# A one-core linear-attention and squared-ReLU block: reordered head loads, merged rest loads, gates moved and woven

## The chip, the core and the metric

The kernel runs on one core of one Trainium2 chip. The metric is device time in microseconds (us) of one execution; lower is better. Everything is bfloat16 in memory, with fp32 sums. The engines that appear below are TensorE (PE; its weight loads are PEld), VectorE (DVE), ScalarE (ACT), GpSimd (POOL) and SyncE (SP). SP and ACT issue DMAs.

## What is computed

x has 2048 tokens of width 448. From the normalised tokens xn two branches are made and multiplied:

```python
xn = _layernorm(x)
# branch A: linear attention, 16 heads of width 28
q, k, v = split(xn @ wqkv)
phi = lambda t: jnp.where(t > 0, t + 1, jnp.exp(t)) + 1e-6
pq, pk = phi(q), phi(k)
kv = einsum("bhsd,bhse->bhde", pk, v)
z = einsum("bhsd->bhd", pk)
o = einsum("bhqd,bhde->bhqe", pq, kv) / (einsum("bhqd,bhd->bhq", pq, z)[..., None] + 1e-6)
s = o @ wo
# branch B: 448 -> 1792 -> 448
h = xn @ w1 + b1
g = silu(relu(h)**2 @ w2 + b2)
return x + s * g
```

## The kernel before, in words

**Tiles.** The 2048 tokens are 16 tiles of 128; four tiles make a group (0 to 3). The width 448 is cut into three full pieces of 128 and a rest of 64. The rest is kept twice, in partitions 0 to 63 and 64 to 127, so that two matmuls of 64 rows can run side by side in the two halves of the array. That is why each weight has a "main" load (three pieces) and "rest" loads (`load_rest`, L396: the same 64 rows of DRAM, copied once into each half by a DMA of its own).

**Units of work on TensorE.** K*i* is the k projection of token tile *i* (L605), Q*g.m* piece *m* of q for group *g* (L615), H*g.f* one of the 14 pieces of h for group *g* (L649), G*i* the gate of tile *i*, from all 14 pieces of h (L957 in halves of the array, L974 in the whole array), S*i* the attention output of tile *i* (L1007). `pe_four` (L523) takes four units a, b, c, d and issues them as pairs: (a, c), (b, d), then both again with the halves exchanged. A gate in such a group takes 14 steps in each half where the others take 4 and 3.

**Between the projections and the end.** R0, R1 are the rests of q (L720). A0 to A3 sum xn times pk over all tokens (L741, L747). `zsums` (L764) adds up pk over the tiles, half of the tiles on POOL and half on VectorE (L769, L781). Z turns that into columns (L794), D makes the denominators (L818). Then ACT takes their logarithm and exponential (lnd L828, rden L832), `spread` writes rden to DRAM (scr) and reads it back in 22 DMAs with each head's row repeated over its 28 partitions, into the space of xT; VectorE multiplies q by it in four instructions (L857 three times, L879 once). V folds the sums with wv (L893), its result goes through VectorE (kvm, L904), M folds that with wo (L919). Every S needs all four multiplies and M.

**Output of a tile.** VectorE adds b2 to the gate (L939), ACT applies silu (L995); gates 14 and 15 get b2 on TensorE and silu straight from PSUM (L956, L947). VectorE multiplies S by the gate (L1012), and the sum with x is on VectorE or POOL (L1017). SP issues the 16 output DMAs.

**Head.** LayerNorm of tile *i* is bn_stats and bn_aggr (L440, L441), two small ACT instructions (L448, L452), xn on VectorE (L459) and the second copy of the rest. Tiles 0 to 3 are transposed on TensorE (L502), with copies out of PSUM on VectorE and ACT (L514, L515); tiles 4 to 15 are transposed by DMAs on SP (L488), two tiles each. The first eight pieces of h of group 0 are accumulated tile by tile as the tiles and the pieces of w1 arrive: six of them in L665, two in L682, and the rests of all eight in L699. They occupy all eight PSUM banks. Dummy matmuls (L1032) run ahead of them.

**What sets the order.** TensorE and SP execute in the order in which the program adds their operations: TensorE's is written out by hand in the strings at the end, SP's is that of the `dma` calls. For ACT, VectorE and POOL a list scheduler in the kernel (`Program.schedule`) chooses the order from estimated durations, due times (`late`) and, for some operations, a choice of engine (`alts`). All engines then run their list strictly in order, with semaphores between them. One `dma` is one DMA instruction.

The strings that give TensorE's order:

```python
run(hs(0, 8, 12) + " P8 H0.12 H0.13 K0 K1 P12 Q0.0 K2 Q0.1 K3 Q0.2 K4 H1.0 H1.1")
run(hs(1, 2, 6) + " XG0,K5,G1,K6 " + hs(1, 6, 10) + " XG2,K7,G3,K8 " + hs(1, 10, 14))
...
run("R0 R1 A3 Z D I0,1,2,3,4,5,6,7 A0 A1 A2 G8 I8 V G9 I9 M")
run("XG10,S0,G11,S4 I10,11 XG12,S1,G13,S5 I12,13 S2 S3 S6 S7 XG14,S8,G15,S12 S9 S10 S13 S14")
run("S11 S15")
```

P is the LayerNorm and transposing of four tiles, I the silu of gates, X one `pe_four` of the units named.

Of the kernel before, what the change touches and what calls it, by code (L numbers as in the profile page):

```python
# [6 lines left out]
ALU = mybir.AluOpType  # L7
AF = mybir.ActivationFunctionType

P = 128  # L10
# [31 lines left out]
class Program:  # L42
# [27 lines left out]
    def schedule(self):  # L70
# [9 lines left out]
        for op in reversed(ops):  # L80
            late = 1e9
            for s in op.succ:
                late = min(late, s.ideal if s.eng == "pe" else s.late)
            for r in op.reads:
                if isinstance(r, Buf):
                    late = min(late, self.writer[r].ideal + 2.5)
            op.late = late - op.dur - LAT[op.eng] if op.prio is None else op.prio
# [40 lines left out]
        while n:  # L128
            best = None
            for e in self.ENGINES:  # L130
# [17 lines left out]
                else:  # L148
                    cands = []
# [12 lines left out]
                    for st, op in cands:  # L162
                        if op.alts:
                            mine = op.dur if op.eng == e else dict(op.alts)[e]
                            others = [(op.eng, op.dur)] + list(op.alts)
                            r = ready(op)
                            if any(
                                max(r, free[x]) + dx < st + mine - 1e-9 for x, dx in others if x != e
                            ):
                                continue  # L170
                            keep.append((st, op, mine))
                        else:
                            keep.append((st, op, op.dur))
# [92 lines left out]
def bass_recurrent_scan__linear_attn_block__dense_activation_squared_relu__prompt_kernel(  # L266
    nc, A_x, A_wqkv, A_wo, B_x, B_w1, B_b1, B_w2, B_b2, out
):
    with ExitStack() as es:
# [35 lines left out]
        zacc = sb("zacc", [P, 2, D], f32)  # L305
# [80 lines left out]
        def load_x(lo, hi, eng="sp"):  # L386
            dma(eng, x_tok[:, lo:hi, :], x_r[:, lo:hi, :], [("x", i) for i in range(lo, hi)], (hi - lo) * P * D * 2)
# [8 lines left out]
        def load_rest(eng, w, src, name, lo, hi, off=0):  # L396
            for i in (0, 1):
                dma(
                    eng, w[64 * i : 64 * i + 64, 3, lo:hi], src[384:448, off + lo : off + hi], [(name, 3 + i)],
                    64 * (hi - lo) * 2,  # L400
                )

        wn = lambda name: [(name, i) for i in range(5)]
# [3 lines left out]
        load_x(1, 2, "act")  # L407
        dma("act", b1r[:, :], B_b1.rearrange("(f p) -> f p", p=P), ["b1r"], F * 2)
        for c in range(3):
            load_main("sp", w_1, B_w1, "w1a", 0, WA, c, c + 1)  # L410
        load_x(2, 4)
# [82 lines left out]
        def pe_transpose(si, pieces):  # L494
            for lo, hi, eng in pieces:
                b = Buf("T")

                def f(e, _, lo=lo, hi=hi, b=b):
# [6 lines left out]
                add(  # L505
                    "pe", f, [("xn", si), "ident"] + ([("xd", si)] if hi == 4 else []), [b], 0.0558 * (hi - lo), mode="128",
                    label=f"T{si}.{lo}",
                )

                def ev(e, eng, lo=lo, hi=hi, b=b):  # L510
# [8 lines left out]
                    eng, ev, [b], [("xT", si, c) for c in range(lo, hi)] + ([("xT", si)] if hi == 4 else []),  # L519
                    0.15 + 0.07 * n if eng == "dve" else 0.18 + 0.107 * n, label=f"eT{si}.{lo}",  # L520
                ).prio = -1 if eng == "act" else None


        def pe_four(a, b, c, d):
            units = (a, b, c, d)
            half = (slice(0, 64), slice(64, 128))
            last = {}
            for us, second in (((a, c), False), ((b, d), False), ((c, a), True), ((d, b), True)):
                whole = us[0][6] > 4
                n = (us[0][6] if second else NF) if whole else 3 if second else 4  # L530
                cuts = [0, 7, n] if whole else [0, n]
                for lo, hi in zip(cuts, cuts[1:]):
# [8 lines left out]
                    reads, banks = [], [u[0] for u in us]  # L541
                    for u in us:
                        reads += [r for r in u[1] if r not in reads]
                    if whole:
                        reads = [r for r in reads if r[0] != "r2" or lo <= r[2] < hi]
                    op = add(
                        "pe", f, reads + (banks if second or lo else []), banks, (hi - lo) * MM(us[0][4]), mode="64",
                        label="+".join(u[5] for u in us) + ("'" if second else "") + (f".{lo}" if lo else ""),
                    )
                    if second and lo == 0:  # L550
                        op.sync = last[id(banks[0])]
                    last[id(banks[0])] = last[id(banks[1])] = op
                if second:
                    for u in us:
                        u[3]()

        def pe_two(a, b):
            half = (slice(0, 64), slice(64, 128))
            first = None
            for second, us in ((False, (a, b)), (True, (b, a))):  # L560
                n = 3 if second else 4

                def f(e, _, us=us, n=n, second=second):
                    for k in range(n):
                        for h in (0, 1):
                            m = us[h][2](e, half[h], k, k == 0 and not second, k == n - 1 and second)
                    return m

                banks = [u[0] for u in us]
                op = add(  # L570
                    "pe", f, a[1] + [r for r in b[1] if r not in a[1]] + (banks if second else []), banks, n * MM(a[4]), mode="64",
                    label=a[5] + "+" + b[5] + ("'" if second else ""),
                )
                if second:
                    op.sync = first
                    for u in us:
                        u[3]()
                first = op
# [97 lines left out]
        def head_rest():  # L676
# [15 lines left out]
            for lo in range(0, HW, 2):  # L692
# [13 lines left out]
                add("pe", f, [("xT", i) for i in range(4)] + [("w1a", 3), ("w1a", 4)] + bs, bs, MM(512), mode="64", label=f"Hr{lo}")  # L706
# [57 lines left out]
        def zsums():  # L764
            def acc(k, eng, tiles):
                for n, i in enumerate(tiles[1:]):
                    add(
                        eng,
                        lambda e, _, n=n, i=i: e.tensor_tensor(  # L769
                            out=zacc[:, k, :], in0=pk[:, tiles[0], :] if n == 0 else zacc[:, k, :], in1=pk[:, i, :], op=ALU.add  # L770
                        ),
                        [("pk", i), ("pk", tiles[0]), ("pk", 11)] if n == 0 else [("pk", i), ("zacc", k)], [("zacc", k)],
                        1.05 if eng == "pool" else 0.64, label=f"z{k}.{i}",
                    )

            acc(0, "pool", list(range(0, 8)))
            acc(1, "dve", list(range(8, 16)))
            for lo, at_, n in ((0, 0, D), (384, D, 64)):
                add(
                    "dve",  # L780
                    lambda e, _, lo=lo, at_=at_, n=n: e.tensor_tensor(  # L781
                        out=zb[:, at_ : at_ + n], in0=zacc[:, 0, lo : lo + n], in1=zacc[:, 1, lo : lo + n], op=ALU.add
                    ),
                    [("zacc", 0), ("zacc", 1)], [("zb", at_)], 0.64 if n == D else 0.15, label="zb",
                )
# [100 lines left out]
        def fold_wv():  # L886
# [14 lines left out]
            for n, lo, hi in ((112, 0, 4), (84, 4, 7)):  # L901
# [7 lines left out]
                )  # L909
# [26 lines left out]
        def g_bias(si, b):  # L936
# [4 lines left out]
            )  # L941

# [56 lines left out]
        final = (13, 15, 14, 11)  # L999

        def s_unit(si):
# [7 lines left out]
            def out_():  # L1009
                gs = gbuf[:, si, :]  # L1010
                add(
                    "dve", lambda e, _: e.tensor_tensor(out=gs, in0=ps(b)[:, 0:D], in1=gs, op=ALU.mult),  # L1012
                    [b, ("g", si)], [("g", si)], 0.625, label=f"mS{si}",
                )
# [5 lines left out]
                dma("sp", o_r[:, si, :], gs, [("out", si)], P * D * 2, [("g", si)])  # L1020
# [31 lines left out]
        warm(6, [("mv", 0)])  # L1052
        bias_cols()
        warm(5, [("rstd", 0)])
        pe_transpose(0, ((0, 2, "dve"), (2, 4, "act")))
        head_part(0, 0, 3)
        pe_transpose(1, ((0, 4, "act"),))
        head_part(1, 0, 1)
        pe_transpose(2, ((0, 4, "act"),))
        head_part(1, 1, 3)  # L1060
        head_part(2, 0, 1)
        pe_transpose(3, ((0, 2, "act"), (2, 4, "act")))
        head_part(2, 1, 3)
        head_part(3, 0, 3)
# [19 lines left out]
        add("pool", lambda e, _: e.tensor_scalar(out=wqh[:, :], in0=w_q[:, 3, 384:448], scalar1=0.5, scalar2=1.0, op0=ALU.mult, op1=ALU.mult), [("wq", 3), ("wq", 4)], ["wqh"], 0.2, label="wqh")  # L1084
# [6 lines left out]
        def run(text):  # L1091
# [32 lines left out]
            if stream:  # L1124
                pe_two(*map(unit, stream))

        hs = lambda g, lo, hi: " ".join(f"H{g}.{i}" for i in range(lo, hi))
        run(hs(0, 8, 12) + " P8 H0.12 H0.13 K0 K1 P12 Q0.0 K2 Q0.1 K3 Q0.2 K4 H1.0 H1.1")
        run(hs(1, 2, 6) + " XG0,K5,G1,K6 " + hs(1, 6, 10) + " XG2,K7,G3,K8 " + hs(1, 10, 14))
        run("Q1.0 H2.0 Q1.1 H2.1 Q1.2 H2.2 K9 H2.3 XG4,K10,G5,K11 " + hs(2, 4, 12) + " XG6,K12,G7,K13")  # L1130
        run("H2.12 H2.13 K14 K15 zs Q2.0 H3.0 Q2.1 H3.1 Q2.2 H3.2 Q3.0 H3.3 Q3.1 H3.4 Q3.2 H3.5 " + hs(3, 6, 14))
        run("R0 R1 A3 Z D I0,1,2,3,4,5,6,7 A0 A1 A2 G8 I8 V G9 I9 M")
        run("XG10,S0,G11,S4 I10,11 XG12,S1,G13,S5 I12,13 S2 S3 S6 S7 XG14,S8,G15,S12 S9 S10 S13 S14")
        run("S11 S15")
# [30 lines left out]
```

## Time and profile before

| | us |
|---|---|
| median of 3 runs | 154.15 (153.26 to 154.41) |
| the profiled execution | 154.46 |
| its span (what the profile covers) | 152.5 |
| TensorE busy | 140.8 |
| VectorE busy | 100.4 |
| ACT busy | 76.0 |
| POOL busy | 23.1 |
| granted TensorE clock, mean | 0.993 |

Times inside the profile count from the span's start. In a group's row stand the source line, the engine, the operation, the operands, the shapes and the count; a wait is given as idle time with the event that ended it. The DMA table gives for each kind of transfer its count, its size and the median time from issue to landing, where the profile has one. SP issues x of tile 0 at 0.79, three pieces of w1 at 1.25 to 2.63, x of tiles 2 and 3 at 2.67, then the rests of w1, its second part, x of tiles 4 to 7 at 6.24, w_k, w_q, b2, x of tiles 8 to 11, and w_2 at 11.84.

### The profile page before, as it was taken

The numbers are of one execution on the slowest core, as the hardware profiler recorded it, in microseconds if no ns is written. First come the engines' busy times: TensorE is split into PE (matmuls) and PEld (weight loads), VectorE is DVE, ScalarE is ACT, GpSimd is POOL, SyncE is SP. The second block draws the span as 40 slices with busy tenths as digits, with TensorE's granted clock in tenths as the row PEclk, the third lists the DMA queues.
The fourth block names the chain that finished last, engine by engine and source line by source line (L and its number), as shares of the span: only waits on it lengthen the run. The fifth ranks groups of instructions, "written<-read, shape, count | busy, mean of one in ns | idle before, by whom it ended". The sixth has DMA issues, their size and how long they took to land.

```text
span 152.5 us, 3300 instructions
## 1 busy us (share of the span) xinstructions
PE 140.8 (92%) x1347; PEld 83.7 (55%) x1347; DVE 100.4 (66%) x218; ACT 76.0 (50%) x150; POOL 23.1 (15%) x57
## 2 busy tenths in 40 slices
PE   6679999799999999999999999989999999999930
PEld 6569457366666556544556666545555455555500
DVE  1545798869798768469979769890055606383690
ACT  3333588789563288427626797683176602110200
POOL 5636000000000000009920000000000000082050
PEclk9999999999999999999999999999999999999997
DMA  4999979880403300300000000001893001013005
GB/s 154 250 262 292 335 244 111 249 195 0 73 0 69 73 0 0 72 1 0 0 4 0 0 4 0 0 4 25 212 189 75 4 0 44 20 60 120 29 31 181
DMA packets 16109, 12.91 MB, mean 85 GB/s; under 512 B 7395, under 2 KB 14815, under 8 KB 16095
## 3 DMA queue, kind: packets, MB, share of 16 engines
q1 hardware_dynamic: 15394, 11.62, 30.1%
q10 hardware_dynamic: 700, 1.09, 3.2%
q8 instruction: 10, 0.16, 0.4%
q14 instruction: 5, 0.03, 0.1%
HBM read 9.23 MB, written 1.90 MB: 73 GB/s over the span
## 4 chain that ended last, share of the span: by engine, by line
PE 80%; DMA 8%; DVE 5%; issue 2%; ACT 1%; ACTq 1%; DVEq 0%
PE pb L957 24%; PE pb L649 23%; PE pb L605 6%; PE pb L1007 6%; PE pb L615 6%; DMA xT<-scr 5%; PE pb L665 4%; PE pb L741 4%; PE pb L1032 3%; DMA xT<-xn 3%; DVE gbuf L1012 2%; DVE pqR L595 1%; PE pb L502 1%; PE pb L682 1%; ACTq L383 1%
## 5 line engine op out<-in xcount | busy, mean ns | idle before, releaser
L649 PE MATMUL pb<-xT,w 64*128 64x512 bf16 x336 | 43.4, 376 | 0.2 <-DVE r L631 0.2
L957 PE MATMUL pb<-w,r 64*128 64x448 bf16 x392 | 39.5, 349 | 0.0
L649 PEld LDWEIGHTS pb<-xT,w 64*128 64x128 bf16 x336 | 21.9, 94 | 14.4 <-DVE r L631 0.7
L957 PEld LDWEIGHTS pb<-w,r 64*128 64x128 bf16 x392 | 20.5, 94 | 16.9 <-issue 0.4
L634 ACT ACTIVATE r<-pb,b1f 128x512 bf16<-128x512 f32 x33 | 21.4, 690 | 7.8 <-PE pb L649 6.8
L639 ACT ACTIVATE r<-r 128x512 bf16<-128x512 bf16 x35 | 20.2, 628 | 0.0
L939 DVE TENSOR_TENSOR gbuf<-pb,b2b 128x448 bf16<-128x448 f32 x14 | 8.2, 618 | 15.1 <-PE pb L957 15.1
L631 DVE TENSOR_SCALAR r<-pb,b1f 128x512 bf16<-128x512 f32 x23 | 16.3, 746 | 2.2 <-PE pb L649 1.6
L605 PE MATMUL pb<-w_k,xT 64*128 64x448 bf16 x112 | 17.5, 349 | 0.0
L1017 POOL TENSOR_TENSOR gbuf<-gbuf,x_tok 128x448 bf16<-128x448 bf16 x6 | 6.2, 1043 | 64.4 <-DVE gbuf L1012 64.4
L583 ACT ACTIVATE pk<-pb 128x448 bf16<-128x448 f32 x16 | 8.2, 543 | 15.1 <-PE pb L605 13.2
L615 PE MATMUL pb<-xT,w_q 64*128 64x512 bf16 x84 | 13.3, 376 | 1.0 <-DMA xT<-xn 1.0
L440 DVE BATCH_NORM_STATS2 st<-x_tok 128x6 f32<-128x448 bf16 x16 | 9.4, 610 | 5.8 <-DMA x_tok<-in_A_x_dram 5.8
L995 ACT ACTIVATE gbuf<-gbuf 128x448 bf16<-128x448 bf16 x14 | 7.1, 571 | 10.6 <-DVE gbuf L939 10.5
L1012 DVE TENSOR_TENSOR gbuf<-pb,gbuf 128x448 bf16<-128x448 f32 x16 | 8.9, 616 | 4.5 <-PE pb L1007 4.5
L1007 PE MATMUL pb<-w_k,pqT 64*128 64x448 bf16 x96 | 10.9, 349 | 0.1
L857 DVE TENSOR_TENSOR pqT<-pqT,xT 128x2048 bf16<-128x2048 bf16 x3 | 3.7, 1225 | 11.0 <-DMA xT<-scr 11.0
L605 PEld LDWEIGHTS pb<-w_k,xT 64*128 64x128 bf16 x112 | 8.1, 94 | 4.4
L595 DVE SCALAR_TENSOR_TENSOR pk<-pb,pk 128x448 bf16<-128x448 f32 x16 | 9.6, 620 | 0.3
L638 DVE TENSOR_TENSOR r<-r 128x512 bf16<-128x512 bf16 x21 | 9.4, 497 | 0.0
L741 PE MATMUL pb<-pk,xn 128*128 128x448 bf16 x48 | 9.3, 353 | 0.0
L665 PE MATMUL pb<-xT,w 128*128 128x128 bf16 x72 | 6.8, 269 | 2.2 <-issue 1.5
(87 smaller groups left out, 143.8 us busy)
## 6 DMA issues: line engine op xcount, KB each, us to landing
out_dram<-gbuf SPq DMA_DIRECT2D x16, 112.0 KB, 1.8
w<-in_B_w_dram SPq DMA_DIRECT2D x1, 1568.0 KB, 12.2
x_tok<-in_A_x_dram SPq DMA_DIRECT2D x3, 448.0 KB, 7.4
w<-in_B_w_dram SPq DMA_DIRECT2D x3, 256.0 KB, 4.2
xT<-scr SPq DMA_DIRECT2D x6, 112.0 KB
w<-in_B_w_dram SPq DMA_DIRECT2D x1, 576.0 KB, 7.4
xT<-scr ACTq DMA_DIRECT2D x5, 112.0 KB
w_o<-in_A_wo_dram SPq DMA_DIRECT2D x1, 392.0 KB, 5.6
```

Of the source, the lines that this page charges most:

```text
L595: lambda e, _: e.scalar_tensor_tensor(out=slot, in0=ps(buf)[0:rows, 0:n], scalar=1.0 + 1e-6, in1=slot, op0=ALU.add, op1=ALU.max),
L605: return e.matmul(ps(b)[:, 0:D], xT[rows, si, c, :], w_k[rows, c, :], start=start, stop=stop)
L615: return e.matmul(ps(b)[:, 0:512], w_q[rows, c, m * P : (m + 1) * P], xT[rows, 4 * g : 4 * g + 4, c, :], start=start, stop=stop,)
L631: return e.tensor_scalar(out=slot, in0=ps(b)[:, 0:512], scalar1=b1f[:, fi : fi + 1], scalar2=0.0, op0=ALU.add, op1=ALU.max)
L634: return e.activation(out=slot, in_=ps(b)[:, 0:512], func=AF.Relu, bias=b1f[:, fi : fi + 1])
L639: return e.activation(out=slot, in_=slot, func=AF.Square)
L649: return e.matmul(ps(b)[:, 0:512], w_1[rows, c, fi * P : (fi + 1) * P], xT[rows, 4 * g : 4 * g + 4, c, :], start=start, stop=stop,)
L665: last = e.matmul(ps(head[fi])[:, i * P : (i + 1) * P], w_1[:, c, fi * P : (fi + 1) * P], xT[:, i, c, :], start=(i == 0 and c == 0), stop= ...
L741: last = e.matmul(ps(b)[:, 0:D], xn[:, si, c * P : (c + 1) * P], pk[:, si, :], start=(si == 0), stop=(si == NT - 1),)
L957: return e.matmul(ps(b)[:, 0:D], r2[rows, fi, si * P : (si + 1) * P], w_2[rows, fi, :], start=start, stop=stop)
L1007: return e.matmul(ps(b)[:, 0:D], w, msb[rows, c, :], start=start, stop=stop)
L1012: "dve", lambda e, _: e.tensor_tensor(out=gs, in0=ps(b)[:, 0:D], in1=gs, op=ALU.mult),
```

## The change

- `load_rest` fills both halves with one DMA: its source names the 64 rows twice (a dimension of 2 with step 0), its destination has 128 partitions.
- The head's loads are reordered: x of tiles 2 and 3 is issued behind the first piece of w1 and ahead of the other two; the bias row b1 behind them on ACT.
- The head's transposes take three pieces a tile; the rests of tiles 0 to 3 are transposed together (TR, `pe_transpose_rests`) and copied out at once. The bias transpose comes behind tile 1's.
- TensorE's order: all of group 0's h ahead of k and q; gates 0 to 3 directly behind; gates 8 to 11 alone in the whole array; A0, A1 ahead of Z and A2 ahead of D.
- `zsums` is on VectorE alone.
- `pe_four` is built of a generator `pair`, and `weave` issues gates 12 to 15 in four pieces of 14 matmuls between the S pairs.
- S14 and S15 are copied out of PSUM by ACT and multiplied from SBUF; the sums with x of tiles 9, 10, 11, 13, 14, 15 are fixed on VectorE; outputs 10 and 11 are issued by ACT.
- In the scheduler: longer due times, and an estimate of what is queued on an engine when one is chosen.

What this makes of the engines' lists, beside what the diff says outright: on VectorE the copy of TR out of PSUM stands behind the bn_stats of tile 4 and ahead of that of tile 5; TR shares a PSUM bank with the second of the two pieces of L682. The second copy of the rest of tiles 6 and 7, which their transposing DMA waits for, stands behind the maxima of q's first two pieces; that of tiles 4 and 5 behind the first four relus. The four multiplies stand behind kvm, gates 8 and 9 and M's copies. All 16 sums with x are on VectorE. On ACT the table load for silu stands ahead of the spread's DMAs, which follow one another.

```diff
-                    late = min(late, self.writer[r].ideal + 2.5)
-            op.late = late - op.dur - LAT[op.eng] if op.prio is None else op.prio
+                    late = min(late, self.writer[r].ideal + 6.0)
+            op.late = late - (4.5 if op.nbytes else op.dur + LAT[op.eng]) if op.prio is None else op.prio
...
         def load_rest(eng, w, src, name, lo, hi, off=0):
-            for i in (0, 1):
-                dma(
-                    eng, w[64 * i : 64 * i + 64, 3, lo:hi], src[384:448, off + lo : off + hi], [(name, 3 + i)],
-                    64 * (hi - lo) * 2,
-                )
+            ld = src.shape[-1]
+            dma(
+                eng, w[:, 3, lo:hi], ap(src, [[0, 2], [ld, 64], [1, hi - lo]], 384 * ld + off + lo), [(name, 3)],
+                128 * (hi - lo) * 2,
+            )
...
         load_x(0, 1)
         load_x(1, 2, "act")
+        load_main("sp", w_1, B_w1, "w1a", 0, WA, 0, 1)
+        load_x(2, 4)
+        load_main("sp", w_1, B_w1, "w1a", 0, WA, 1, 2)
+        load_main("sp", w_1, B_w1, "w1a", 0, WA, 2, 3)
         dma("act", b1r[:, :], B_b1.rearrange("(f p) -> f p", p=P), ["b1r"], F * 2)
-        for c in range(3):
-            load_main("sp", w_1, B_w1, "w1a", 0, WA, c, c + 1)
-        load_x(2, 4)
         load_rest("sp", w_1, B_w1, "w1a", 0, WA)
...
+        def pe_transpose_rests():
+            b = Buf("T")
+            def f(e, _):
+                v = ps(b)[:, :].bitcast(bf)
+                for si in range(4):
+                    last = e.transpose(v[:, si * P : (si + 1) * P], xn[:, si, 384:512], ident[:, :])
+                return last
+            add("pe", f, [("xd", i) for i in range(4)] + ["ident"], [b], 0.0558 * 4, mode="128", label="TR")
...
+            add("act", ev, [b], [("xT", i) for i in range(4)], 0.6, alts=[("dve", 0.43)], label="eTR")
...
+        def pe_four(a, b, c, d):
+            one, two = pair(a, c), pair(b, d)
+            n1, n2 = (2 if u[6] > 4 else 1 for u in (a, b))
+            for _h in (0, 1):
+                for p, n in ((one, n1), (two, n2)):
+                    for _i in range(n):
+                        next(p)
...
         def zsums():
-            acc(0, "pool", list(range(0, 8)))
-            acc(1, "dve", list(range(8, 16)))
+            for i in range(1, NT):
+                for lo, at_, n in ((0, 0, D), (384, D, 64)):
...
-                )
+                ).prio = 0
...
-        final = (13, 15, 14, 11)
+        final = (9, 13, 10, 14, 11, 15)
+        by_act = (14, 15)
...
-                dma("sp", o_r[:, si, :], gs, [("out", si)], P * D * 2, [("g", si)])
+                dma("act" if si in (10, 11) else "sp", o_r[:, si, :], gs, [("out", si)], P * D * 2, [("g", si)])
...
+        run(hs(0, 8, 14) + " K0 K1 K2 Q0.0 K3 Q0.1 XG0,Q0.2,G1,K4 P8 XG2,K5,G3,K6 " + hs(1, 0, 4))
+        run("P12 K7 H1.4 Q1.0 H1.5 Q1.1 H1.6 Q1.2 H1.7 " + hs(1, 8, 14) + " K8 H2.0 XG4,K9,G5,K10 " + hs(2, 1, 5))
+        run("XG6,K11,G7,Q2.0 H2.5 Q2.1 H2.6 Q2.2 " + hs(2, 7, 11) + " H2.11 K12 H2.12 K13 H2.13 K14 H3.0 K15 zs")
+        run("H3.1 Q3.0 H3.2 Q3.1 H3.3 Q3.2 H3.4 H3.5 " + hs(3, 6, 14))
+        run("R0 R1 A3 A0 A1 Z A2 D I0,1,2,3,4,5,6,7 V G8 G9 M G10 G11")
+        weave(
+            "G12|G13 S0|S4 G12|G13 S0|S4 S1|S5 G12|G13 S1|S5 S2|S6 G12|G13 S2|S6 G14|G15 S3|S7 G14|G15 S3|S7 S8|S12 G14|G15"
+            " S8|S12 S9|S13 G14|G15 S9|S13 S10|S14 S11|S15 S10|S14 S11|S15"
+        )
```

## The prediction

> **What bounds the kernel now.** I read the page first (busy shares, slices), then the chain of work that ended last, the timeline at head, normaliser and tail, then the DMA table and DMA windows.
>
> ```profile
> PE 140.8 (92%) x1347; PEld 83.7 (55%) x1347; DVE 100.4 (66%) x218; ACT 76.0 (50%) x150; POOL 23.1 (15%) x57
> PE   6679999799999999999999999989999999999930
> DMA  4999979880403300300000000001893001013005
> ```
>
> TensorE bounds it: 92% busy. Only its 11.7 us of idle time can be won without removing matmuls, and the change removes none worth counting. The idle time lies in the first five slices and the last two. DMA is full in just those first five.
>
> ```profile
> 24.19 4.34 DMA xT<-xn
> 28.53 0.05 issue
> 28.57 0.39 PE pb L615
> ...
> 109.95 7.61 DMA xT<-scr
> ...
> 144.82 2.75 DVE gbuf L1012 x5
> ```
>
> The chain follows TensorE except for a wait for the transposes of tiles 4 to 7 (TensorE could have gone on at 27.34 by its issue steps, so 1.2 us are lost), the spreading of the normaliser, and VectorE's last multiplies.
>
> ```profile
> 7.97 2.08 PE L665 MATMUL pb<-xT,w 128*128 128x128 bf16 x18 [1.52 <-issue]
> 13.71 2.21 DVE L440 BATCH_NORM_STATS2 st<-x_tok 128x6 f32<-128x448 bf16 x4 [1.76 <-DMA x_tok<-in_A_x_dram]
> 14.21 1.98 PE L665 MATMUL pb<-xT,w 128*128 128x128 bf16 x30
> 17.42 1.04 PE L699 MATMUL pb<-xT,w 64*128 64x512 bf16 x8
> ```
>
> In the head the first real matmul waits for the third piece of w1 (issued 2.2, 5.6 us to landing). Tiles 4 to 7 of x land at 13.65. Equal matmuls take 115 ns each at 7.97 and 66 ns at 14.21.
>
> ```profile
> w<-in_B_w_dram SPq DMA_DIRECT2D x1, 1568.0 KB, 12.2
> xT<-scr SPq DMA_DIRECT2D x6, 112.0 KB
> xT<-scr SPq DMA_DIRECT2D x1, 64.0 KB, 4.0
> DMA  9999999999999999999998885442111000000000
> GB/s 358 346 352 352 329 352 329 352 323 358 323 358 323 346 335 335 352 317 370 299 329 275 257 276 191 143 137 72 48 54 36 24 18 24 24 24 18 6 0 0
> ```
>
> The last two lines are the DMA window 18 to 24 us. Sixteen engines together move some 340 GB/s; at the end one lagging engine alone moves 24 GB/s, and w2 lands at 24.0 only when it is done. The landing column is filled for transfers whose outer dimension is a multiple of 16 (the 64 KB one has 16 rows) and empty for the others (112 KB is 28 rows). The trace's completion records behind it say why: a 16-row transfer ends in 16 marks, 28 rows in 15, 12 in 13, 8 in 9, 4 in 5. So the outer dimension is dealt evenly over the largest number of engines up to 16 that divides it (28 over 14, 4 over 4), with one mark for all the missing ones.
>
> **The change part by part.** Times are those of the profiled execution (span 152.5, time 154.46); it lies 0.31 above the median of 154.15, to which I apply the sum.
>
> *A. Loads of the first weights.* x of tiles 2, 3 is now issued ahead of w1's pieces 2 and 3, so piece 3 takes x's place in the queue: 8.6 instead of 7.8, and the first matmul waits for it. T1, T2 have three transposes instead of four, TR adds four; about even. At 115 and 66 ns per matmul 0.65 us late at 7.97 leaves 0.3 at L699. Bounds 0 to 0.65. It is hidden under B, so 0 in the sum, 0.3 if B is not there.
>
> *B. The rest loads (load_rest).* Two transfers of 64 rows become one whose source is [2, 64, n] with step 0 and whose destination has 128 rows. An even deal has to divide both outer dimensions, and 2 is the most. The trace before has no transfer with unequal outer dimensions: one bound is two engines, the other is sixteen (no cost). I take two, since sixteen can't deal out a source of two.
> The Trainium skill ("DMA: Bandwidth & Descriptors", section "Why a DMA increments its semaphore by 16 and not by 1") says that the number of engines is the largest up to 16 that divides the slowest dimension of both patterns, here 2; the trace agrees as far as its records go (28 rows, 15 marks). By that rule the sum is the one below, by sixteen engines the first rival's.
> On SP's queue behind SP's x, w1: 262 KB, 197 KB, then 115 KB each for k and q. Two engines at 24 GB/s take 5.5 + 4.1 + 2.4 + 2.4 = 14.4 us; sixteen at 300 GB/s take 2.3. Two rings are 12.1 us longer and everything dealt over sixteen waits for them. SP's issues saved (four of some 0.6 us by 12 us) don't count, the queue isn't issue-bound.
> - x of tiles 4 to 7: 13.65 + 9.6 - 1.5 = 21.7. VectorE is in order: bn_stats of tile 4 waits for it, and right behind stands the copy of TR out of PSUM (that copy frees the bank of the last w1 group of L682 and feeds L699). 21.7 + 0.6 + 0.45 = 22.75. Behind those stand two more bn_stats and two xn, so its first relus start some 1.0 late. Before, TensorE needed 10.66 from that place (16.68) to 27.34: now 22.75 + 10.66 + 1.0 = 34.4.
> - w2, which gates 0 to 3 now need at this place: 21.9 + 12.1 = 34.0 if the two engines aren't the lagging one, 24.0 + 12.1 = 36.1 if they are. Middle 35.2 with landing; that is later than TensorE's 34.4.
> Gate 0 starts at 35.2, and what TensorE then has left is what it had at 28.57. Cost +6.6, in which the 1.2 us wait at 28.57 is already won. Bounds: +3.5 (the other engines, done sooner, leave these two more: x at 20, gate 0 at 32), and +12.5 at 15.8 GB/s an engine, the page's mean (11.62 MB in 30.1% of 16 engines' span): 21.8 us for 14.4.
>
> *C. h first, gates 0 to 3 at once.* No price beside B. The transposes of tiles 6, 7 are now issued after VectorE's copy behind q's maxima, some 13 us after the first relus: 38, landing 3.0 to 4.9 later; k6 needs them 9.4 after gate 0, at 44.6. Without B they land at 36.2 to 38.1 and are needed at 37.0: 0 to 1.1, 0.3.
>
> *D. pk sums on VectorE, other planner costs.* 15 adds in 9 us where VectorE had 7 adds in 5.9, plus 0.8, and POOL 8.1. While POOL adds, VectorE's own add takes 1.24 to 1.34, afterwards 0.61; three squares 2.76, else 1.09: 3.3 us come back. TensorE, busy from 28.57 to 97, hides it. From gate 7 to the second q rest I count on VectorE 6 q at 0.91, 5 k at 0.85, 12 relus at 0.69, 8 adds at 0.58 and 1.2 for gates: 23.8 us in some 25.6; if that cover breaks, the eight adds, 4.6 us, lie bare in part. I put 0.15; bounds 0 to 0.8. At nothing: the bias transpose moved behind T1 (needed first at the relus), kvm ahead of the multiplies, v's merged load (2.4 us on two rings near 40, needed near 110), the table load (1.28) ahead of ACT's spread issues (scr takes 2.1 to land).
>
> ```profile
> 102.27 0.69 ACT L828 ACTIVATE lnd<-pb,eps 128x512 f32<-128x512 f32 x1
> 116.26 1.23 DVE L857 TENSOR_TENSOR pqT<-pqT,xT 128x2048 bf16<-128x2048 bf16 x1 [1.66 <-DMA xT<-scr]
> 118.53 0.68 DVE L879 TENSOR_TENSOR pqR<-pqR,xT 128x1024 bf16<-128x1024 bf16 x1
> ```
>
> *E. Normaliser later.* From lnd the third multiply ends 15.2 later, the fourth can end at 15.9; the transfers fill the DMA meanwhile (0.9 of it), so ACT's unbroken issues win nothing. All from the start of A3: A3, A0 to A2, Z, D are 11.7, lnd 11.9, scaled q 27.8. TensorE comes to the first S pair at 11.7 + 1.3 (V) + 4 x 2.65 (gates 8 to 11) + 0.95 (M) + 1.35 (half of gates 12, 13) = 25.9. It waits 1.8 (bounds 0.9 to 2.5). Three waits go (0.36 for Z, 0.42 for D, 0.42 for M, now behind A, V and gates). Then 20.3 of matmuls: last one at 48.1, before at 146.37 - 98.86 = 47.5. +0.6.
>
> *F. Tail.* Before, 146.37 to 152.5 is 6.1: six outputs 0.49 apart on SP behind a POOL add. Now VectorE has after the last matmul one multiply 0.6, two from SBUF and four adds 0.3 each: 2.4, two outputs on ACT, then 0.1 and 2.26 (last issue 150.24 to the end). 4.8: -1.3. Bounds -0.6 to -1.6.
>
> Sum: 6.6 + 0.15 + 0.6 - 1.3 = +6.05. 154.15 + 6.05 = 160.2.
>
> **The rivals.**
> *Sixteen engines (not slower).* The merged loads spread as before; then +0.3 - 1.2 + 0.3 + 0.15 + 0.6 - 1.3 = -1.15: 153.0, spread 151.8 to 154.3. For it: no row shows unequal dimensions. Against: the marks for 28, 12, 8 and 4. It decides where gate 0 starts: below 29.1 the change wins.
> *Two engines, and TensorE slows down in the pause.* It is idle from 17.1 to 22.75. In the head it ran 115 ns a matmul for 6.0 us after 7.97, behind a pause of 1.5. If that comes back, 6.0 x (1 - 66/115) = 2.6: TensorE reaches gate 0 at 37.0, +1.8: 162.0. Against: no pause after 14 in this trace was long enough to show it.
> The Trainium skill ("TensorE: Matmul & The Clock Gate", Part 1) states that after an idle window of about 3.4 us the clock halves; no run here shows it yet, and it speaks for this rival.
> *The wait before the first S pair is not there* (multiplies done sooner): -1.8 on either, 158.4.
>
> **How the numbers follow.** Two engines at full clock 0.47, with the slow clock 0.29, without the S wait 0.04, sixteen engines 0.20. Predicted 160.2. The two-engine cases alone reach from 157 (a smaller B) to 164 (a larger one, or the slow clock); with half of the sixteen-engine case the range is 153 to 164. About 1% is what a measurement of this kernel can tell. The two-engine cases are all slower, 0.80; of the sixteen-engine 0.20, faster 0.07, within 1% 0.11, slower 0.02.
>
> **What would show it.** B: rest loads with 3 marks, x of tiles 4 to 7 landing past 20, bn_stats waiting for it, TensorE idle inside L697 (before: L682), w2 past 33, a long stretch of 48 GB/s in the DMA windows. A: first L680 (before: L665) at about 8.6. C: no wait at k6. E: a wait of 1 to 2.5 us at the first S pair, none before Z, D, M. F: under 5 us after the last matmul. I am wrong if x of tiles 4 to 7 lands at 13 to 14; then all of B goes.

## The result and the profile after

The changed kernel takes 159.16 us (median of 4 runs, 158.22 to 160.34), the kernel before 153.86 beside it (4 runs). The ratio is 1.035, 95% interval 1.027 to 1.043: slower, as forecast, and 1.0 below the 160.2 of the prediction. The profiled execution took 158.22 with a span of 156.5; it is the shortest of the four (spans of the others: 157.2, 157.6, 158.6). In all ratios of this document, runs more than 1.5% above the fastest of the same kernel are left out, so a ratio can lie below the quotient of the medians.

From the page of the changed kernel come the same busy shares and slices that were shown of before; PEclk is the granted clock of TensorE in tenths.

```profile
PE 139.8 (89%) x1319; PEld 81.1 (52%) x1319; DVE 105.3 (67%) x238; ACT 74.1 (47%) x146; POOL 8.6 (6%) x44
PE   6785079989999999999999999999999995999970
PEclk9999659999999999999999999999999999999999
DMA  5854439921960600070300000000004990031133
```

TensorE has an empty slice (15.6 to 19.6 us), a lower clock in it and right behind it, and a half slice at 129. DMA, which was full through the first five slices of before, is now half idle there, and most of w2 moves in slices 7 and 8.

The chain of waits of the changed kernel (start, us, what):

```profile
5.14 14.52 DMA x_tok<-in_A_x_dram
19.68 0.63 DVE st L453
20.31 0.33 DVE xT L547
20.69 1.46 PE pb L697 x3
...
31.93 0.99 ACT pk L598 x2
32.92 2.82 PE pb L968 x28
...
122.69 8.01 DMA xT<-scr
130.74 0.70 DVE pqR L888
...
151.19 1.19 DVE gbuf L1034 x2
```

x of tiles 4 to 7 is issued at 5.14 and is 14.5 us under way. bn_stats of tile 4 (L453) waits for it, the copy of TR (L547) stands right behind it, and the second half of L697 waits for that copy. This is the path that part B named, as far as L697. The completion marks of this transfer show the two engines at work: fourteen of its sixteen marks stand by 12.65, the last two come at 19.65. What ends last ahead of gate 0 (L968, 32.92) is ACT's work on pk, at 32.9; w2 had landed at 32.8, so two chains end there within 0.1 us. TensorE's timeline shows what it costs, and what the pause does to the clock:

```profile
7.23 1.17 PE L680 MATMUL pb<-xT,w 128*128 128x128 bf16 x18 [1.12 <-DVE xn L472]
13.01 0.81 PE L697 MATMUL pb<-xT,w 128*128 128x512 bf16 x3
20.69 1.46 PE L697 MATMUL pb<-xT,w 128*128 128x512 bf16 x3 [6.88 <-DVE xT L547]
22.08 1.73 PE L714 MATMUL pb<-xT,w 64*128 64x512 bf16 x8
...
32.92 2.82 PE L968 MATMUL pb<-w,r 64*128 64x448 bf16 x28 [0.39 <-ACT pk L598]
```

6.88 us of waiting; then three matmuls take 1.46, where the same number took 0.81 ahead of the pause, and L714 takes 1.73 (before: 1.04 for the same eight). The trace's clock records say half clock from 16.7 to 23.5.

The DMA window 18 to 24 us of the changed kernel (before it moved 340 GB/s through its first half):

```profile
DMA  3998999742111111111111111112339468375656
GB/s 96 251 233 275 323 370 346 257 161 90 54 48 42 42 48 48 48 48 48 48 48 48 48 48 48 48 42 102 131 120 215 90 90 108 72 114 96 137 155 191
```

48 GB/s is two engines at the 24 GB/s at which a single lagging engine ran in the trace of before. All five merged loads end in 3 completion marks; their landings are 12.96 (w1a), 18.67 (w1b), 22.9 (k), 26.5 (q) and 46.4 (v). The window 30 to 33 us has w2's end: from 31.2 to 32.5 at most two engines' worth is moved; the rise behind that is the first transposes.

```profile
GB/s 311 253 300 260 236 225 183 154 111 106 79 85 73 82 72 65 43 48 48 48 36 48 48 48 48 36 48 48 34 31 34 41 34 34 205 294 280 297 287 277
```

Span by stages, from the same places in the timelines of three profiles: gate 0's first matmul, the first matmul of A3, the end of the last matmul, the end of the span. The column e1 is the changed kernel with the old loads (experiment below).

| stage | before | changed | e1 | changed - before | forecast |
|---|---|---|---|---|---|
| start to gate 0 | 28.57 | 32.92 | 27.94 | +4.35 | +6.6 (B) |
| gate 0 to A3 | 70.29 | 70.38 | 70.43 | +0.09 | +0.15 (D) |
| A3 to last matmul | 47.51 | 48.42 | 48.32 | +0.91 | +0.6 (E) |
| last matmul to end | 6.1 | 4.7 | 4.7 | -1.4 | -1.3 (F) |
| span | 152.5 | 156.5 | 151.4 | +4.0 | +6.05 |

### The profile page after: what moved, and what is told of

It is laid out like the page before. It is cut to its first block, busy times and chain, and to the rows that moved or that the text cites. A ratio compares the mean times of both kernels' runs of the same rounds, so it can differ in the third digit from the quotient of the medians.

```text
span 156.5 us, 3233 instructions
## 1 busy us (share of the span) xinstructions
PE 139.8 (89%) x1319; PEld 81.1 (52%) x1319; DVE 105.3 (67%) x238; ACT 74.1 (47%) x146; POOL 8.6 (6%) x44
## 4 chain that ended last, share of the span: by engine, by line
PE 72%; DMA 15%; SPq 5%; DVE 3%; ACT 1%; issue 1%; ACTq 0%; DVEq 0%
PE pb L664 23%; PE pb L968 20%; DMA x_tok<-in_A_x_dram 9%; PE pb L620 7%; PE pb L1019 7%; PE pb L756 6%; PE pb L630 5%; DMA xT<-scr 5%; SPq L395 5%; PE pb L735 1%; DMA scr<-rden 1%; PE pb L714 1%; PE pb L762 1%; PE pb L697 1%; DVE gbuf L1034 1%
## 5 line engine op out<-in xcount | busy, mean ns | idle before, releaser
L664 PE MATMUL pb<-xT,w 64*128 64x512 bf16 x336 | 42.0, 376 | 0.0
L968 PE MATMUL pb<-w,r 64*128 64x448 bf16 x336 | 34.7, 349 | 0.4 <-ACT pk L598 0.4
L664 PEld LDWEIGHTS pb<-xT,w 64*128 64x128 bf16 x336 | 20.8, 94 | 15.7 <-DVE r L646 0.5
L968 PEld LDWEIGHTS pb<-w,r 64*128 64x128 bf16 x336 | 18.7, 94 | 14.1 <-ACT pk L598 0.9
L649 ACT ACTIVATE r<-pb,b1f 128x512 bf16<-128x512 f32 x31 | 20.2, 688 | 9.3 <-PE pb L664 8.3
L646 DVE TENSOR_SCALAR r<-pb,b1f 128x512 bf16<-128x512 f32 x25 | 17.8, 745 | 2.2 <-PE pb L664 2.1
L620 PE MATMUL pb<-w_k,xT 64*128 64x448 bf16 x112 | 17.8, 349 | 0.0
L453 DVE BATCH_NORM_STATS2 st<-x_tok 128x6 f32<-128x448 bf16 x16 | 9.5, 610 | 10.3 <-DMA x_tok<-in_A_x_dram 10.3
L630 PE MATMUL pb<-xT,w_q 64*128 64x512 bf16 x84 | 14.9, 376 | 0.0
L598 ACT ACTIVATE pqT<-pb 128x512 bf16<-128x512 f32 x12 | 6.7, 598 | 10.0 <-PE pb L630 5.9
L461 ACT ACTIVATE vep<-mv,eps 128x2 f32<-128x2 f32 (+1 forms) x10 | 2.9, 295 | 17.0 <-DVE mv L454 17.0
L985 PE MATMUL pb<-w,r 128*128 128x448 bf16 x56 | 10.9, 353 | 0.0
```

Of the source, the lines that this page charges most:

```text
L598: "act", lambda e, _: e.activation(out=slot, in_=ps(buf)[0:rows, 0:n], func=AF.Exp), [buf, "actw"],
L620: return e.matmul(ps(b)[:, 0:D], xT[rows, si, c, :], w_k[rows, c, :], start=start, stop=stop)
L630: return e.matmul(ps(b)[:, 0:512], w_q[rows, c, m * P : (m + 1) * P], xT[rows, 4 * g : 4 * g + 4, c, :], start=start, stop=stop,)
L646: return e.tensor_scalar(out=slot, in0=ps(b)[:, 0:512], scalar1=b1f[:, fi : fi + 1], scalar2=0.0, op0=ALU.add, op1=ALU.max)
L649: return e.activation(out=slot, in_=ps(b)[:, 0:512], func=AF.Relu, bias=b1f[:, fi : fi + 1])
L664: return e.matmul(ps(b)[:, 0:512], w_1[rows, c, fi * P : (fi + 1) * P], xT[rows, 4 * g : 4 * g + 4, c, :], start=start, stop=stop,)
```

## The experiments

**e1_two_dma: only the merged loads undone.**

```diff
-            dma(eng, w[:, 3, lo:hi], ap(src, [[0, 2], [ld, 64], [1, hi - lo]], ...), [(name, 3)], ...)
+            for i in (0, 1):
+                dma(eng, w[64 * i : 64 * i + 64, 3, lo:hi], src[384:448, ...], [(name, 3 + i)], ...)
```

> The changed kernel with the old load_rest: two loads of 64 rows instead of one of [2, 64, n]; every other instruction keeps its place on its engine. Theory (the merged loads ran on two engines and held x of tiles 4 to 7 and w2 up): the rest loads end in 16 marks, x lands at 13 to 14.5, SP's issues are again some 0.5 us apart, w2 lands by 25, TensorE's 6.9 us of waiting shrink to about 1 and the clock stays full. The head of the changed kernel was 2.85 us ahead of the kernel before at that place (13.83 instead of 16.68), so gate 0 starts at 25 to 27: 150.5 us (149.5 to 152.5), ratio to the kernel before 0.97 to 0.99. First rival (the head's lead is lost to something else, the merged loads cost only what was forecast): 153 to 154.3, ratio about 1. Second rival (the order of the stages costs it, not the merged loads): 157 to 159 as the changed kernel.

Measured: 153.3 us (12 runs, 151.18 to 155.20), ratio 0.991 (0.987 to 0.996). Timeline of TensorE:

```profile
8.34 2.08 PE L680 MATMUL pb<-xT,w 128*128 128x128 bf16 x18 [2.68 <-DMA w<-in_B_w_dram]
...
27.94 2.86 PE L968 MATMUL pb<-w,r 64*128 64x448 bf16 x28
...
126.47 0.74 PE L1019 MATMUL pb<-w_k,pqT 64*128 64x448 bf16 x6 [1.70 <-DVE pqR L888]
```

The 6.88 us are gone, the rest loads end in 16 marks, and x of tiles 4 to 7 lands at 13.2. So the whole slowdown is the merged loads: everything else in the change makes the kernel about 0.9% faster. The ratio lies between my theory (0.97 to 0.99) and the first rival (about 1), and its interval touches the theory's; the 150.5 was too low: it took the head's lead of 2.85 us in the changed kernel for a gain of the new load order. Here L680 starts at 8.34 and runs 116 ns a matmul, so the lead came with the merged loads (w1's third piece lands at 7.14 with them, at 8.25 here; probably because fourteen engines have less to move) and with the clock.

**e2_merged_in_before: only the merged loads, in the kernel before.** The edit is that of e1 reversed.

> The kernel before with the merged load_rest alone; nothing else moves on any engine but SP's list of loads. Theory (two engines): rest loads with 3 marks and a stretch of 48 GB/s, x of tiles 4 to 7 at 19 to 20, w2 at about 33, gate 0 at 33 to 34: 158.5 to 161 us, ratio 1.03 to 1.045. Rival (the order of the stages costs it): 153.5 to 154.5, ratio 1.00.

Measured: 161.95 us (4 runs), ratio 1.056 (1.051 to 1.061), more than the 158.5 to 161 that I expected; 3 marks, and again a stretch of 48 GB/s. VectorE's and TensorE's timelines:

```profile
19.67 2.21 DVE L440 BATCH_NORM_STATS2 st<-x_tok 128x6 f32<-128x448 bf16 x4 [9.35 <-DMA x_tok<-in_A_x_dram]
```
```profile
24.09 5.36 PE L649 MATMUL pb<-xT,w 64*128 64x512 bf16 x29 [8.45 <-DVE r L631]
```

By the medians the merged loads alone cost 8.3 us in the old order and 5.9 in the new one (5.6% and 4.4% of the time of before by the ratios). In the old order VectorE holds the first relus behind the same bn_stats, and the 29 matmuls behind the pause take 5.36 instead of 3.41, at a half clock that the records give from 17.8 to 28.1. The gates come only at 42.06 there, long behind w2 (32.8): in this order it is the wait for x alone, which brings TensorE to the first matmuls that need the transposes of tiles 4 to 7 at 36.11 instead of 28.57, 7.5 of the 7.6 by which the spans differ.

**e6_source_2x32 and e7_source_8x8: is it the repeated rows or the dimension?** Two loads of 64 rows as in e1, but the source is written with 2, or 8, as its slowest dimension, and no row is read twice. The rest weights then stand in wrong rows, so these two kernels do the same work and give other numbers:

```diff
-  src[384:448, off + lo : off + hi]
+  ap(src, [[ld, 2], [2 * ld, 32], [1, hi - lo]], 384 * ld + off + lo)    # e6; 8 and 8 in e7
```

> e1_two_dma, each rest load of 64 rows read through a source of [2, 32, n] (rows in another order, so the rest weights stand in wrong rows and the numbers that come out differ; sizes, counts and bytes are those of e1_two_dma, and no row is read twice). Theory (the smaller of the two slowest dimensions deals out the engines): 3 marks for each, a stretch of 48 GB/s, x of tiles 4 to 7 at 18 to 20, 157 to 161 us. Rival (reading the rows twice by a step of 0 makes the load slow): 16 marks, x at 13 to 14.5, 151.5 to 155.

> As e6_source_2x32 with a source of [8, 8, n] (rows again in another order). Theory: 9 marks, eight engines, the rest loads' tail on them is a quarter as long as on two (14.4 / 4 = 3.6 us), x of tiles 4 to 7 at 13.5 to 16, 151.5 to 156 us. Rival (any source with a second dimension of rows is slow): as e6_source_2x32.

Measured, one run each: e6 158.86 with 3 marks for every rest load, e7 155.99 with 9 marks. Timeline and DMA window (18 to 24) of e6:

```profile
21.23 1.46 PE L698 MATMUL pb<-xT,w 128*128 128x512 bf16 x3 [7.18 <-DVE xT L548]
```
```profile
GB/s 44 86 156 172 137 78 215 346 382 364 317 233 96 48 48 48 42 48 48 48 48 48 48 48 48 42 48 48 42 48 48 48 72 90 131 125 131 78 102 119
```

With nothing read twice the load is as slow as the merged one (x of tiles 4 to 7 lands at 20.2), so the step of 0 is not the cause: the 2 is. With 8, x lands at 14.2, bn_stats of tile 4 starts at 15.2, and TensorE waits for nothing within the six matmuls that are L697 in the changed kernel. The Trainium skill ("DMA: Bandwidth & Descriptors", section "Why a DMA increments its semaphore by 16 and not by 1") has the engines as the largest number up to 16 that divides the slowest dimension of both sides; the marks of 2, 8 and 64 rows (3, 9, 16) agree with it.

**e3_busy_in_pause and e4_planner_knows: what sets gate 0 in the changed kernel?**

```diff
+                if fi == HA:     # e3: zeros added to a bank in use, 90 times
...
+                    add("pe", keep, [head[HA]], [head[HA]], 0.0, mode="128", label="keep")
```
```diff
-                128 * (hi - lo) * 2,
+                128 * (hi - lo) * 2 * 15 // 2,     # e4: bytes of load_rest as the planner counts them
```

> The changed kernel with 90 matmuls of zeros (adding 0 to a bank in use) in TensorE's pause after 13.8, so that it is never idle there; all else keeps its place. The clock should stay full through the pause, and the matmuls from 20.7 to 23.5 take half the time, 1.4 us less. Theory (gate 0 waits for w2, at 32.8): TensorE comes to gate 0 at 31 and waits 1.5 there, the time is the changed kernel's within 0.4 (158.5 to 159.4). Rival (TensorE's own chain from x to gate 0 is the bound): 1.4 less, 157.5 to 158.

> The changed kernel, whose planner is told that a merged load takes 7.5 times as long: VectorE's and ScalarE's work on tiles 4 to 7 now stands behind the copy of TR and the first relus instead of ahead of them; TensorE's and SP's orders are the same. Theory (w2 sets gate 0): no wait of TensorE inside L697, shorter waits later for the rest loads of w1b, k and q (18.7, 22.9, 26.5), and gate 0 still at 32.5 to 33: 158.3 to 159.4. Rival (x of tiles 4 to 7 on VectorE's queue is the bound): gate 0 at 29 or before, 155 to 156.5.

Measured: e3 158.68 (ratio 1.034, 1.027 to 1.041), e4 160.89 (1.048, 1.043 to 1.054). TensorE in e3, then in e4:

```profile
20.67 0.82 PE L697 MATMUL pb<-xT,w 128*128 128x512 bf16 x3 [0.59 <-DVE xT L547]
...
33.00 2.83 PE L978 MATMUL pb<-w,r 64*128 64x448 bf16 x28 [0.73 <-DMA w<-in_B_w_dram]
```
```profile
33.69 2.82 PE L968 MATMUL pb<-w,r 64*128 64x448 bf16 x28 [3.94 <-DMA w<-in_B_w_dram]
...
133.34 0.74 PE L1019 MATMUL pb<-w_k,pqT 64*128 64x448 bf16 x6 [2.26 <-DVE pqR L888]
```

In e3 the clock stays full through the pause, but the next matmuls wait for VectorE's relus (0.92), and gate 0 starts at 33.00 behind w2 (landed 32.87): no gain that can be measured. In e4 TensorE comes to gate 0 at 29.75 and waits 3.94 us for w2. So w2 holds gate 0 at this place even when TensorE's chain comes sooner, and the half clock of the pause was almost hidden. e4 is slower than the 158.3 to 159.4 that I expected; its trace shows two parts of that: w2 landed 0.9 later than in the changed kernel, and the wait at the first S pair is 2.26, behind which the records show one stretch of half clock (134.0 to 137.4, worth about 1.7 us).

**e5_norm_sooner: the wait at the first S pair.**

```diff
-        run("R0 R1 A3 A0 A1 Z A2 D I0,1,2,3,4,5,6,7 V G8 G9 M G10 G11")
+        run("R0 R1 A3 A0 Z A1 D A2 I0,1,2,3,4,5,6,7 V G8 G9 M G10 G11")
```

> e1_two_dma with the normaliser's two stages moved up by one token sum: A3 A0 Z A1 D A2 instead of A3 A0 A1 Z A2 D. One token sum is 3.1 us of TensorE. Theory (the wait of 1.7 to 1.8 us at the first S pair is the spread of the normaliser come late): that wait goes, none over 0.2 comes ahead of Z, D or V, and the time falls by 1.7 against e1_two_dma, to 151.6, ratio to the kernel before 0.98. Rival (VectorE's own order of gates, kvm and multiplies sets the first S pair): the wait stays above 1, 153.0 to 153.5.

Measured: 151.88 (12 runs, 151.06 to 153.12), ratio 0.991 (0.987 to 0.994). The wait at S0 is gone, so the late normaliser was its cause. Another takes part of its place:

```profile
110.89 1.49 PE L902 MATMUL pb<-at,w_v 128*112 128x64 bf16 x28 [0.63 <-ACT at L775]
```

The 151.6 nearly came, the ratio of 0.98 did not: the median is 1.4 below e1's, but the two ratios are the same, so a gain in time is not shown. What such a wait can cost beyond its length stands in the trace of e7, which has e1's order: after a wait of 2.24 at S0, TensorE's windows give

```profile
125.00:132.00 7.00, 4.85 (x34) 0.76 0.02 4
```

a granted clock of 0.76. The records say half from 127.4 to 130.8, which is worth about 1.7 us; it is part of why e7 is slower than e1. The waits of 1.70 (e1) and 1.79 (changed kernel) at the same place were followed by full clock.

**e9_busy_head: the wait for w1.**

```diff
         pe_transpose(0, ((0, 2, "dve"), (2, 3, "act")))
+        warm(36)
```

> e1_two_dma with 36 more matmuls on zeros between the transposes of tile 0 and the first matmul on w1, in the 2.7 us in which TensorE waits there for w1; all else keeps its place. Theory (that wait costs the half clock that e1_two_dma shows from 8.1 to 14.9): the clock stays full, equal matmuls take 66 ns from the start, TensorE is 2.6 us sooner at L697, and gate 0 waits for nothing longer than 0.8: 151.0 us, ratio 0.975 to 0.987. Rival (the loads set the head): the lead is given back as waits for the rest of w1, x of tiles 4 to 7 and w2, 152.5 to 153.5.

Measured: 152.01 (12 runs, 150.58 to 155.57), ratio 0.990 (0.986 to 0.994).

```profile
8.66 1.17 PE L680 MATMUL pb<-xT,w 128*128 128x128 bf16 x18 [1.02 <-DMA w<-in_B_w_dram]
...
17.51 3.41 PE L664 MATMUL pb<-xT,w 64*128 64x512 bf16 x29 [0.65 <-DVE r L646]
```

The clock stays full: 65 ns a matmul where e1 took 116. TensorE is 1.75 us sooner at L664 (e1: 19.26), and the profiled span 1.7 shorter; of the 2.6 expected, part comes back as a new wait of 0.65 for VectorE's relus. So the mechanism is shown, but the ratio is e1's within the intervals and above the 0.975 to 0.987 expected: as with e5, a gain in time is not shown by this run alone.

**e8_both and e10_gate_before_v: the pieces put together.** e8 is e5 with e9's `warm(36)`; e10 also writes `G8 V G9` for `V G8 G9`.

> e1_two_dma with both edits: A3 A0 Z A1 D A2 of e5_norm_sooner and the 36 matmuls on zeros of e9_busy_head. If the two gains lie in different places (the head, the first S pair) they add: e5 took 1.4 off e1 and e9 1.3, so 150.6 us, ratio 0.98 to 0.985, no half clock ahead of the tail. If the gain of e9 was only a lucky clock, it stays at e5's 151.9.

> e8_both with gate 8 ahead of V: the 0.63 us that TensorE waits there for the copy of the last token sum lies under a gate. Theory: 0.5 less than e8_both, 150.1. Rival: kvm and M come later on VectorE and the multiplies behind them, so that a wait at M or at the first S pair takes its place: 150.6 or more.

Measured: e8 151.02 (6 runs), ratio 0.984 (0.980 to 0.988); e10 149.88 (6 runs), ratio 0.972 (0.967 to 0.977). From the page of e10:

```profile
PE 140.1 (95%) x1355; PEld 87.8 (60%) x1355; DVE 104.0 (71%) x236; ACT 74.9 (51%) x148; POOL 8.6 (6%) x44
PE   6989799999999999999999999999999999999970
```

With both edits the ratio falls from 0.991 to 0.984, and the intervals of e1 and e8 overlap only at their ends; whether the two gains add is not shown, since neither could be measured alone. e10 is faster than both kernels. Between the head and the tail its TensorE waits nowhere for more than 0.2 us. Against e8 the median fell by 1.1 where 0.5 was expected; the profiled spans differ by 1.8, of which about 1.0 is w1's third piece landing sooner in that one execution (7.87 instead of 8.94).

## Why the prediction was right, and where its sizes were off

- **B, two engines.** The mechanism is right: 3 marks, the stretch at 48 GB/s, bn_stats ahead of the copy of TR, TensorE idle inside L697, w2 late for gate 0. Two links differ. At gate 0 w2 (32.8) and the chain over TensorE and ACT (32.9) came together, where 35.2 and 34.4 were forecast; and SP, whose issues I had put at nothing, was held up and issued w2 at 22.0 instead of 11.8 (last section). Undoing B gives back 5.9 us of medians (5.1 of spans), adding it to the kernel before costs 8.3.
- **B, its size, is the term that was off: +6.6 forecast, +4.35 measured.** (The two traced executions differ by less than the medians, which leave some 5.7 for B as an estimate: 5.3, and 0.4 that the other stages won.) Landings were forecast at 21.7 (x) and 35.2 (w2, a middle) and came at 19.7 and 32.8. The rate was right: from 12.96 to 18.67 each of the two engines moved its share of w1b's main load (37 KB) and half of the rest load (98 KB), 24 GB/s. What failed is the starting point: I added the two engines' extra work to landings of before, at which all sixteen engines shared some 340 GB/s (21 each) and one lagged. Counting instead what each of the two has to move behind w1's third piece (landed 7.1) gives an estimate that fits better: 295 KB up to x of tiles 4 to 7 and 589 KB up to w2 are 12.3 and 24.5 us at 24 GB/s, so 19.4 and 31.6. The lower bound that I gave (x at 20, gate 0 at 32) was near that.
- **The slow clock.** The second rival's mechanism was there (half clock from 16.7 to 23.5), its price was not: it lay under the wait for w2 (e3). The row that I took for its size was misread: in the trace of before the dummy matmuls ahead of the pause already take 112 ns each (36 in 4.02 us), and the record of full clock begins at 13.8, so the 115 ns after 7.97 were no effect of the pause.
- **A.** L680 at 8.6 was forecast; without the merged loads it starts at 8.34 (e1). With them it starts at 7.23, which I had not expected.
- **C.** No wait at k6; the second transpose was issued at 37.3 and landed at 40.4, where 38 and 41 to 43 were forecast.
- **D, E, F.** +0.09, +0.91 and -1.4 in the table, against +0.15, +0.6, -1.3. The wait at the first S pair was forecast at 1.8 and is 1.79; none is left ahead of Z, D or M; the tail was forecast at 4.8 and is 4.7.
- **The rest (sixteen engines).** That rival's sum, -1.15 on 154.15, is a ratio of 0.993; e1 measures 0.991 (0.987 to 0.996), and its span is 1.1 below that of before. The terms beside B are right as a sum too.
- The median rose by 5.3 where the two profiled executions differ by 3.8: that of before (154.46) lies above all of its four runs here, that of the changed kernel (158.22) is the shortest of its four. The traces of e3 and e4, with the same order on TensorE up to 13 us, have half clock in the head from 7.8 to 11.2, which the profiled execution of the changed kernel does not have; that may be what its other runs had, but they were not traced.

## What to carry to other kernels

Before folding two DMAs into one, look at the slowest dimension of both sides: a leading 2 put the whole load on two engines here, and what was queued behind it waited for those two, because each of them had a share of it. Price that by what those two engines have to move in all, from the moment they start. When a transfer is late, follow what stands behind its consumer in an in-order queue, and look for the second arrival (here w2) before pricing the first. A wait of TensorE of about 2 us can cost more than its length, since the clock dropped behind two such waits (2.24 in e7, 2.26 in e4); matmuls on zeros in the head's wait kept the clock full (e9).

## What was not expected of the hardware

SP's own issues get slow while the two engines are behind. SP's timeline in the changed kernel:

```profile
5.14 4.18 SPq L395 DMA_DIRECT2D x_tok<-in_A_x_dram  x1
9.37 3.74 SPq L395 DMA_DIRECT2D w_k<-in_A_wqkv_dram  x2
13.14 5.40 SPq L395 DMA_DIRECT2D w_q<-in_A_wqkv_dram  x2
...
21.99 0.43 SPq L395 DMA_DIRECT2D w<-in_B_w_dram  x1
```

One issue of x takes 4.18 us (0.58 in e1), and w2 is issued at 22.0 instead of 11.8. I had only counted the waiting of transfers, not of SP. Whether w2 would have landed sooner if it had been issued on time was not tried. By the estimate above, hardly: of the 25.4 us from 7.1 to 32.5, where the DMA windows have the two engines done with w2, their 589 KB fill 24.5 at 24 GB/s, so they can have stood idle for less than 1 us.

Once the clock has been full, and up to the last matmul, the half clock comes in pieces of 3.41 us or a multiple of it in all traces here, and what counts seems to be how the idle time falls into such pieces: 2.24 us idle in one piece was followed by half clock (e7), 3.94 us lying across two (e4, ahead of gate 0) was not. The Trainium skill ("TensorE: Matmul & The Clock Gate", Part 1) has a free-running window of 3413 ns and half clock after one idle window; the length agrees, but here a window idle for two thirds was enough.
